# A list scheduler inside a kernel: a charge on vector work that overlaps GpSimd, and two GpSimd prices raised

## The chip, the cores and the metric

The kernel runs on one core of a Trainium2 chip. The metric is the device time of one execution in microseconds, from the first to the last instruction and what lies around them.

## The reference

Block-sparse attention, whose output is the input of a feed-forward layer with a rational function in place of an activation:

```
scores = scale * q @ k.T                    # batch 4, heads 8, sequence 768, head dim 64
mask   = own and neighbour blocks of 32, first and last block, 3 sampled blocks per row block
attn   = softmax(where(mask, scores, -1e9)) @ v
x      = attn as (3072, 512)
h      = x @ w_in                           # w_in 512 x 2048
P      = a0 + a1*h + a2*h^2 + a3*h^3
Q      = 1 + |b0|*|h| + |b1|*h^2
out    = (P / (Q + 1e-6)) @ w_out           # w_out 2048 x 512
```

`w_in` and `w_out` come as 64-bit floats.

## The kernel before

The 3072 tokens are cut into 12 chunks of 256 (three to a batch), the 2048 hidden values into 8 slices of 256. A **unit** is one chunk and one slice: 96 in all. The order of units is written out: slices 0 to 3 of chunk 0, slices 0 to 7 of chunk 1, slices 4 to 7 of chunk 0, and from there chunk by chunk. A unit's matmuls with `w_in` are lines 1036 to 1038 (function `into`, result `ph`), three passes since both sides are split into a high and a low half. ScalarE and VectorE then make the rational function (lines 1043 to 1081). Its value `gh` is written by VectorE at line 1071, and its remainder `gl` at line 1081. TensorE multiplies them with `w_out` (lines 1093, 1095 and 1099, result `acc`). So line 1093 of unit n waits for line 1071 of unit n.

Attention is done in parts of two row blocks (56 parts): scores on TensorE (line 817), mask and maximum on VectorE (829), exponentials on ScalarE (848), transposes of them (894), product with `v` (940), normalisation (966), transposes of the result (978), and its split into `xh` and `xl` (984 to 989). Four row-block pairs make a chunk. The first unit of a chunk needs the chunk's last `xl`.

The weights are decoded on the way. Each 64-bit word is loaded as two integers. A first copy of the high word (`convert`, line 437, by the helper at lines 150 to 154) goes to VectorE, ScalarE or GpSimd. Then VectorE alone does three integer steps (`pack1` to `pack3`, lines 441, 444, 447). For `w_out` (16 pieces, loaded at line 427 on SyncE's queue into two buffers `wl`) a high half `wo_h` (`out_high`), its remainder `wo_l` (`out_low`, line 461) and a short form `wo_b` (`out_short`) follow. For `w_in` (16 pieces) there are the largest value (378), the scale (344 to 356), the scaled copy `dw` (`scaled`), the high half (`high`) and the remainder (`low`, line 519). All of this is needed by the 12th unit.

What stands where in each engine's queue is set by a scheduler that runs while the program is built (`issue`). Every piece of work is an `Op` with an engine, or several to choose from (`among`), and a price in nanoseconds for each. The scheduler keeps a planned time for each engine, takes the operation that can start first, adds its price, and writes the instruction. Each engine then runs its queue in that order, whatever the real times are. Among engines, the home engine is preferred unless another can start earlier by a margin (`other`). While TensorE has nothing to do in the plan and no unit has been accumulated yet, `fill` writes a matmul without use (line 162) to its queue.

Of the kernel before, what the change touches and what calls it, by code (L numbers as in the profile page):

```python
# [24 lines left out]
def kernel(  # L25
# [71 lines left out]
    VE, SC, PO, TE, SY = "DVE", "Activation", "Pool", "PE", "SP"  # L97
# [17 lines left out]
    class Op:  # L115


        def __init__(self, eng, price, run, after=(), prio=0.0, takes=(), uses=(), unit=None, behind=None):
            self.alt = eng if isinstance(eng, dict) else None
            self.engs = list(eng) if self.alt else [eng]  # L120
            self.eng, self.price, self.run, self.prio, self.unit = self.engs[0], price, run, prio, unit
            self.after, self.behind = [a for a in after if a is not None], behind
            self.takes, self.uses, self.rings = list(takes), list(takes) + list(uses), {}
            for s in self.takes:
                self.rings[s.ring] = self.rings.get(s.ring, 0) + 1
            for s in self.uses:
                s.left += 1
            self.next, self.at, self.work = [], dict.fromkeys(self.engs, 0.0), 1.0
            plan.append(self)

    plan = []
# [10 lines left out]
    def among(key, home, **prices):  # L142

        d = {{"ve": VE, "sc": SC, "po": PO}[n]: p for n, p in prices.items()}
        return {home: d[home], **(d if key in ALT else {})}
# [18 lines left out]
    def issue(ahead):  # L164
# [11 lines left out]
        now = dict.fromkeys(todo, 500.0)  # L176
        clock, dma, lanes = -1.0, 0.0, [0.0] * 8
        busy, window, warm = {}, 0, False
        for n, o in enumerate(plan):
            o.n, o.wait = n, len(o.after) + (o.behind is not None)  # L180
            for a in o.after:
                a.next.append(o)
            if o.behind:
                o.behind.next.append(o)
            if not o.wait:
                for e in o.engs:
                    todo[e].append(o)
        left = len(plan)
        fsh = 0.8
        other = {VE: 500, SC: 534.0, PO: 243.0}  # L190
        unit_of = {VE: nc.vector, SC: nc.scalar, PO: nc.gpsimd}
        slack, fend, f00, fgap = 21.0, 80000, 3000, 0
        while left:
# [22 lines left out]
            if isinstance(price, list):  # L216
                for ns, size in price:
                    t = max(t, lanes.pop(0) if e == SY else t) + ns
                    dma = max(dma, t + 650) + size / 360.0
                    if e == SY:  # L220
                        lanes.append(dma + 900)
                end = dma + 900
            elif e == TE:
                f0 = max(now[e], f00)
                while f0 < fend and not accs:
                    tick(f0)
                    f = 213 if warm else 427
                    if f0 + f + fgap > t:
                        break
                    fill()  # L230
                    work_of(f0, f, 1.0)
                    f0 += f
                tick(t)
                if now[e] < fend and not accs:
                    w = window
                    x0 = w * 3413
                    for _ in range(2):
                        if not warm or t - x0 < 700 or busy.get(w, 0.0) >= fsh * (t - x0):
                            break
                        fill()  # L240
                        work_of(t, 213, 1.0)
                        t += 213
                if not warm:
                    price *= 2 if price > 1100 or price < 500 else 1.8
                work_of(t, price, o.work)
                end = t = t + price
            else:
                end = t = t + price
            now[e] = t
            o.end = end  # L250
# [146 lines left out]
    def weights():  # L397
# [21 lines left out]
        def one(prio, kind, u, x, before):  # L419
# [48 lines left out]
            before[kind] = o0  # L468
            w = [s_w] if kind else []
            o = Op(among("c", SC, sc=520, po=588, ve=335), 0, convert, [o0], prio, takes=w, uses=wl)  # L470
            if not kind:
                begun[u, x] = o
            o = Op(VE, 335, pack1, [o], prio, uses=w)
# [2 lines left out]
            if not kind:  # L476
                freed[u, x] = o
            if kind:
                o1 = Op(among("o", SC, sc=520, po=588, ve=335), 0, out_high, [o], prio, uses=w)
                o2 = Op(among("p", PO, po=1225, ve=602), 0, out_low, [o1] + homes(x), prio, uses=w)  # L480
                o3 = Op(among("q", SC, sc=520, po=588, ve=335), 0, out_short, [o] + homes(x), prio, uses=w)
                out_ready[x] = [o2, o3]
                decoded.append(o3)
                decoded.append(o2)
                return o2
# [10 lines left out]
    def w_scaled(u, prio, group, sums):  # L496
# [10 lines left out]
        for x in range(NCC):  # L507
            def three(x):
# [10 lines left out]
                    eng.tensor_tensor(out=wi[:, x, u, 1], in0=d["w"], in1=wi[:, x, u, 0], op=ALU.subtract)  # L519

                a = Op(among("s", PO, po=671, ve=396, sc=613), 0, scaled, [o], prio, takes=[s_ws])
                a = Op(among("h", SC, sc=520, po=588, ve=335), 0, high, [a], prio, uses=[s_ws])
                a = Op(among("l", PO, po=1113, ve=602), 0, low, [a], prio, uses=[s_ws])
                in_ready.setdefault(u, []).append(a)
                decoded.append(a)
            three(x)
# [719 lines left out]
```

## Time and profile before

| | |
|---|---|
| median of three runs | 829.0 us (827.88 to 829.31) |
| profiled execution: time, span from first to last instruction | 828.6 us, 826.8 us |
| TensorE busy | 770.6 us (93%) |
| VectorE busy | 674.9 us (82%) |
| ScalarE busy | 569.7 us (69%) |
| GpSimd busy | 107.5 us (13%), all in the first 220 us |

The profile page cuts the span into 40 slices of 20.7 us. TensorE's busy share is lowest in the sixth, VectorE's is highest from there to the eleventh, and from the twelfth on TensorE is at 9 tenths or more in every slice. The page's row for TensorE's granted clock shows less than full speed only in the fifth to seventh slice.

### The profile page before, as it was taken

To read this page: it belongs to the slowest core of one execution; us is meant where nothing else is said; L and a number is where in the kernel's file an instruction comes from. 1 tells how busy PE (TensorE), PEld (TensorE's weight loads), DVE (VectorE), ACT (ScalarE), POOL (GpSimd) and SP (SyncE) were. 2 spreads that over 40 slices of the span, in tenths; PEclk is the share of its full clock that TensorE was granted. 3 is DMA by queue.
4 is the path that set the end of the run, shared out by engine and by line. 5 is a ranking of instruction groups with operands and counts; after the bars stand their busy time and mean duration, and the time that the engine had idled before them with its cause. 6 is when DMAs were issued, how large, how long until landed. Compare 5 with 4: busy or idle time off the path is not lost.

```text
span 826.8 us, 27468 instructions
## 1 busy us (share of the span) xinstructions
PE 770.6 (93%) x10859; PEld 557.3 (67%) x10943; DVE 674.9 (82%) x1580; ACT 569.7 (69%) x1264; POOL 107.5 (13%) x149
## 2 busy tenths in 40 slices
PE   8798918898999999999999999999999999999997
PEld 4556605676677768677777767677777767767774
DVE  2788999899988885788878884887888886887886
ACT  2676777677866769677576759676676758766563
POOL 3547485613100000000000000000000000000000
PEclk9999969899999999999999999999999999999999
DMA  7988874537566957545636757635555436220000
GB/s 210 242 220 238 233 231 138 163 87 189 142 154 165 214 162 194 162 123 162 160 108 164 191 145 196 173 96 157 144 151 149 117 111 182 76 65 2 1 26 26
DMA packets 224416, 121.29 MB, mean 147 GB/s; under 512 B 62624, under 2 KB 214048, under 8 KB 224288
## 3 DMA queue, kind: packets, MB, share of 16 engines
q1 hardware_dynamic: 223136, 115.34, 51.6%
q0 software_dynamic: 1152, 4.19, 1.6%
q8 instruction: 86, 1.41, 0.8%
q14 instruction: 42, 0.34, 0.1%
HBM read 108.47 MB, written 11.01 MB: 145 GB/s over the span
## 4 chain that ended last, share of the span: by engine, by line
PE 81%; DVE 7%; DMA 4%; issue 3%; ACT 2%; POOL 2%; SPq 1%; ACTq 0%; POOLq 0%; DVEq 0%
PE acc L1093 11%; PE ph L1036 9%; PE acc L1095 9%; PE acc L1099 9%; PE ph L1037 9%; PE ph L1038 9%; PE m L817 7%; PE av L940 6%; PE m L894 6%; PE acc L162 3%; DMA vg<-in_v_dram 2%; PE m L556 2%; DMA wl<-in_moe_w_out_dram 1%; PE m L978 1%; POOL wo_h L154 1%
## 5 line engine op out<-in xcount | busy, mean ns | idle before, releaser
L1037 PE MATMUL ph<-xl,wi 128*128 128x256 f16 x768 | 210.5, 274 | 3.1 <-DVE xl L989 3.1
L1036 PE MATMUL ph<-xh,wi 128*128 128x256 f16 x768 | 210.9, 275 | 1.4 <-DVE tt L1053 1.4
L1038 PE MATMUL ph<-xh,wi 128*128 128x256 f16 x768 | 210.7, 274 | 0.0
L1043 ACT ACTIVATE sq<-ph,fc 128x512 f32<-128x512 f32 x96 | 65.9, 687 | 112.6 <-PE ph L1038 112.4
L1093 PE MATMUL acc<-wo_h,gh 128*128 128x512 f32 x384 | 114.5, 420 | 18.7 <-DVE gh L1071 18.0
L848 ACT ACTIVATE pr<-pr,st 128x256 f32<-128x256 f32 x224 | 110.7, 501 | 14.3 <-DVE st L860 14.3
L1060 DVE SCALAR_TENSOR_TENSOR ab<-sq,absb,ab 128x512 f32<-128x512 f32 x96 | 73.2, 763 | 37.1 <-ACT ab L1057 36.9
L829 DVE CUSTOM_DVE_ANT_1 pr<-m,bias 128x256 f32<-128x256 f32 x224 | 83.2, 418 | 22.3 <-PE m L817 22.1
L1099 PE MATMUL acc<-wo_b,gl 128*128 128x512 bf16 x368 | 95.4, 379 | 3.4 <-issue 2.1
L1095 PE MATMUL acc<-wo_l,gh 128*128 128x512 bf16 x316 | 86.5, 384 | 4.6
L1036 PEld LDWEIGHTS <-wi 128*128 128x128 f16 x768 | 75.9, 99 | 21.4 <-issue 5.1
L1071 DVE SCALAR_TENSOR_TENSOR gh<-tt,par,rr 128x512 fp32r<-128x512 f32 x96 | 72.3, 753 | 19.8 <-ACT rr L1067 11.2
L1093 PEld LDWEIGHTS acc<-wo_h,gh 128*128 128x128 f32 x384 | 66.0, 191 | 32.7 <-issue 19.6
L150 ACT ACTIVATE pT<-m 128x512 f32<-128x512 f32 x112 | 64.1, 596 | 34.0 <-PE m L894 32.7
L1037 PEld LDWEIGHTS <-wi 128*128 128x128 f16 x768 | 75.6, 98 | 12.7 <-issue 0.2
L1038 PEld LDWEIGHTS <-wi 128*128 128x128 f16 x768 | 75.5, 98 | 12.6 <-issue 3.4
L1047 ACT ACTIVATE tt<-ph,par,fc 128x512 f32<-128x512 f32 x96 | 74.8, 779 | 0.3 <-DVE gl L1081 0.2
L1050 DVE TENSOR_TENSOR tt<-tt,sq 128x512 f32<-128x512 f32 x96 | 66.9, 697 | 9.4 <-ACT tt L1047 9.4
L1057 ACT ACTIVATE ab<-ph,fc 128x512 f32<-128x512 f32 x96 | 65.6, 683 | 11.2 <-DVE tt L1077 10.5
L1077 DVE SCALAR_TENSOR_TENSOR tt<-tt,par,ab 128x512 f32<-128x512 f32 x96 | 72.2, 752 | 0.5
L894 PE MATMUL m<-ident,pr 128*128 128x128 f32 x448 | 69.6, 288 | 2.9 <-ACT kt L150 2.3
L1053 DVE SCALAR_TENSOR_TENSOR tt<-ph,fc,tt 128x512 f32<-128x512 f32 x96 | 71.4, 744 | 0.8
(130 smaller groups left out, 1221.7 us busy)
## 6 DMA issues: line engine op xcount, KB each, us to landing
vg<-in_v_dram SPq DMA_DIRECT2D x312, 64.0 KB, 2.9
vg<-in_v_dram SPq DMA_DIRECT2D x88, 192.0 KB, 3.6
kall<-ks SPq DMA_DIRECT2D x138, 64.0 KB, 1.9
wl<-in_moe_w_out_dram SPq DMA_DIRECT2D x16, 512.0 KB, 4.8
vg<-in_v_dram SPq DMA_DIRECT2D x12, 512.0 KB, 5.1
kall<-ks SPq DMA_DIRECT2D x23, 256.0 KB, 3.7
ldq<-in_q_dram SPq DMA_DIRECT2D x20, 256.0 KB, 3.4
out_dram<-ld SPq DMA_DIRECT2D x20, 256.0 KB, 2.4
```

The costliest lines, as they stand in the source:

```text
L829: nc.vector.tensor_tensor_reduce(out=prs[x][:, e, g].rearrange("p (s r) -> p s r", r=BLK), in0=h["sp"][g][:, e], in1=add.rearrange("p (s o ...
L848: nc.scalar.activation(out=prs[x][:, e, g], in_=prs[x][:, e, g], func=AF.Exp, scale=SCALE, bias=st[:, 12 + y:13 + y], accum_out=st[:, 16 + ...
L894: nc.tensor.transpose(pp[:, jj * P:(jj + 1) * P], pr[:, e, g, kt:NS * BLK:2], ident)
L1036: nc.tensor.matmul(o, wh, xh[:, :, cc], start=(cc == 0), stop=False)
L1037: nc.tensor.matmul(o, wh, xl[:, :, cc], start=False, stop=False)
L1038: nc.tensor.matmul(o, wl, xh[:, :, cc], start=False, stop=(cc == NCC - 1))
L1047: nc.scalar.activation(out=d["tt"], in_=d["ph"], func=AF.Identity, scale=d["cst"][:, 3:4], bias=par[:, 2:3])
L1060: nc.vector.scalar_tensor_tensor(out=d["ab"], in0=d["sq"], scalar=absb[:, 1:2], in1=d["ab"], op0=ALU.mult, op1=ALU.add)
L1071: nc.vector.scalar_tensor_tensor(out=d["gh"], in0=d["tt"], scalar=par[:, 0:1], in1=d["rr"], op0=ALU.add, op1=ALU.mult)
L1093: nc.tensor.matmul(acc, g, wo_h[:, f], start=(new and e == 0), stop=False)
L1095: nc.tensor.matmul(acc, g, wo_l[:, f], start=False, stop=False)
L1099: nc.tensor.matmul(acc, g, wo_b[:, f], start=False, stop=(last and e == 1))
```

## The change

The scheduler gets a list of GpSimd's planned operations on weights (`pooled`), each with a factor `drag`: 0.36 for copies, 0.62 for subtractions. An operation planned for VectorE gets longer by the factor times its overlap with such an operation (`dragged`). When GpSimd's operation is planned after VectorE's, VectorE's planned time is moved by the same product. Two prices on GpSimd rise: that of `out_high` from 588 to 1050, and that of `out_low` from 1225 to 1400. No instruction of the program changes by itself. What changes is which engine takes a weight operation, and the order in every queue.

```diff
+        pooled = []
+        def dragged(t, price):
+            more = 0.0
+            for a, b, drag in pooled:
+                more += drag * max(0.0, min(b, t + price) - max(a, t))
+            return more
...
             else:
+                if e == PO and o.drag:
+                    while pooled and pooled[0][1] < t - 20000:
+                        pooled.pop(0)
+                    pooled.append((t, t + price, o.drag))
+                    late = o.drag * max(0.0, min(now[VE], t + price) - max(t, last_dve))
+                    now[VE] += late
+                if e == VE:
+                    last_dve = t
+                    price += dragged(t, price)
                 end = t = t + price
...
             o = Op(among("c", SC, sc=520, po=588, ve=335), 0, convert, [o0], prio, takes=w, uses=wl)
+            o.drag = 0.36
...
-                o1 = Op(among("o", SC, sc=520, po=588, ve=335), 0, out_high, [o], prio, uses=w)
-                o2 = Op(among("p", PO, po=1225, ve=602), 0, out_low, [o1] + homes(x), prio, uses=w)
+                o1 = Op(among("o", SC, sc=520, po=1050, ve=335), 0, out_high, [o], prio, uses=w)
+                o2 = Op(among("p", PO, po=1400, ve=602), 0, out_low, [o1] + homes(x), prio, uses=w)
+                o2.drag = 0.62
...
                 a = Op(among("s", PO, po=671, ve=396, sc=613), 0, scaled, [o], prio, takes=[s_ws])
+                a.drag = 0.36
                 a = Op(among("h", SC, sc=520, po=588, ve=335), 0, high, [a], prio, uses=[s_ws])
                 a = Op(among("l", PO, po=1113, ve=602), 0, low, [a], prio, uses=[s_ws])
+                a.drag = 0.62
```

The changed file has more lines, so a line of the kernel before stands some 20 lines later in it: 1071 becomes 1093, 1093 becomes 1115.

How many weight operations each engine gets, counted in the built programs:

| operation | VectorE | ScalarE | GpSimd |
|---|---|---|---|
| first copy, `w_out` (`dw<-wl`) | 2, now 0 | 5, now 7 | 9, now 9 |
| first copy, `w_in` (`wi<-wo_l`, `wi<-wo_b`) | 3, now 2 | 6, now 5 | 7, now 9 |
| scaled copy (`dw<-wi,scw`) | 4, now 3 | 0, now 2 | 12, now 11 |
| high half of `w_out` (`wo_h<-dw`) | 2, now 1 | 6, now 9 | 8, now 6 |
| remainder of `w_out` (`wo_l<-dw,wo_h`) | 1, now 0 | 0 | 15, now 16 |

TensorE's queue gets 143 fills for 135. From the 25th unit on, the order of VectorE's and ScalarE's queue is that of before.

**TensorE, before the third unit's line 1093.** In the kernel before, the third unit's product with `w_out` stands right behind the second's:

```order
L556 MATMUL m_101<-ident,ldq 128x128 x4
L1099 LDWEIGHTS gl
L1099 MATMUL acc<-wo_b,gl 128x512
...
L1093 MATMUL acc<-wo_h,gh 128x512 x4
...
L894 MATMUL m_103<-ident,pr 128x128 x4
L894 MATMUL m_102<-ident,pr 128x128 x4
L894 MATMUL m_101<-ident,pr 128x128 x4
...
L940 MATMUL av<-vg_112,pT 32x64 x32
L339 MATMUL m_103<-ident,sums 128x128
```

In the changed kernel (line 916 is what 894 was, 962 what 940 was, 839 what 817 was):

```order
L1121 LDWEIGHTS gl
L1121 MATMUL acc<-wo_b,gl 128x512
L916 MATMUL m_103<-ident,pr 128x128 x4
L962 MATMUL av<-vg_112,pT 32x64 x32
L916 MATMUL m_103<-ident,pr 128x128 x8
L962 MATMUL av<-vg_110,pT 32x64 x32
...
L962 MATMUL av<-vg_112,pT 32x64 x32
L357 MATMUL m_102<-ident,sums 128x128
L839 MATMUL m_103<-kx,qt 32x96
...
L1000 MATMUL m_102<-ident,xn 128x128 x4
L1115 MATMUL acc<-wo_h,gh 128x512 x4
```

Three parts' transposes and products with `v`, one part's scores and the transposes of four blocks' output have moved ahead of the third unit's line 1093.

**VectorE, before the fifth unit's `gh`.** The names: `dw` and `wi` are weights being decoded, `fc` the coefficients of a slice, `xl` the low half of a chunk's input. Before:

```order
L1010 TENSOR_SCALAR fc<-wscale,sc_1035,par 128x2 x2
L989 SCALAR_TENSOR_TENSOR xl_119<-m_103,xscale,xh_118 128x512
L152 CAST wo_h<-dw 128x512
L461 TENSOR_TENSOR wo_l<-dw,wo_h 128x512
L154 TENSOR_SCALAR dw<-wi,scw 128x512 x2
L1060 SCALAR_TENSOR_TENSOR ab<-sq,absb,ab 128x512
L1050 TENSOR_TENSOR tt<-tt,sq 128x512
L1053 SCALAR_TENSOR_TENSOR tt<-ph,fc,tt 128x512
L154 TENSOR_SCALAR dw<-wl 128x512
L441 TENSOR_SCALAR dw<-dw 128x512
L1060 SCALAR_TENSOR_TENSOR ab<-sq,absb,ab 128x512
L1071 SCALAR_TENSOR_TENSOR gh<-tt,par,rr 128x512
```

In the changed kernel:

```order
L465 SCALAR_TENSOR_TENSOR wi<-wo_b,wi 128x512
L465 SCALAR_TENSOR_TENSOR wi<-wo_l,wi 128x512
L459 TENSOR_SCALAR wi<-wi 128x512
L1082 SCALAR_TENSOR_TENSOR ab<-sq,absb,ab 128x512
L462 SCALAR_TENSOR_TENSOR wi<-wo_b,wi 128x512
L1075 SCALAR_TENSOR_TENSOR tt<-ph,fc,tt 128x512
L465 SCALAR_TENSOR_TENSOR wi<-wo_b,wi 128x512
L851 ISA pr,st<-m_103,bias 128x256
L851 ISA st 128x1
L851 ISA pr,st<-m_101,bias 128x256
L851 ISA st 128x1
L1093 SCALAR_TENSOR_TENSOR gh<-tt,par,rr 128x512
```

The fifth unit's `gh` has moved ahead of the coefficients, of two `w_out` pieces' steps and of a third's first. From the fourth unit's `gh` to the fifth's there are 64 VectorE instructions before and 19 now. The `xl` of the second chunk stands 52 instructions earlier, ahead of the fourth unit's `gh`.

**SyncE's queue, the last two loads of `w_out` pieces.** Before (`kall<-ks` are loads of key blocks for a later part, `vg` of value blocks):

```order
L427 DMA wl<-in_moe_w_out_dram 128x1024
L912 DMA vg_110<-in_v_dram 48x8x128
L914 DMA vg_110<-in_v_dram 16x8x128
L915 DMA vg_110<-in_v_dram 16x8x128
...
L427 DMA wl<-in_moe_w_out_dram 128x1024
```

In the changed kernel:

```order
L445 DMA wl<-in_moe_w_out_dram 128x1024
L934 DMA vg_113<-in_v_dram 48x8x128
L936 DMA vg_113<-in_v_dram 16x8x128
L937 DMA vg_113<-in_v_dram 16x8x128
...
L797 DMA kall<-ks 128x4x128
L733 TENSOR_LOAD ix
...
L803 DMA kall<-ks 128x128
L445 DMA wl<-in_moe_w_out_dram 128x1024
```

The second of these is the sixteenth piece's load. It now stands behind these key loads of a part (one at line 797, six at line 803), which came after it before. The fourteenth piece's load stands behind two such groups, of which it was ahead before. In all, three groups stand ahead of the sixteenth load for one before.

## Rows read from the trace of the kernel before

**Rows 1.** Busy time of each engine in two stretches of the span.

```profile
core 0: us, PE busy (x) PEld busy (x) DVE busy (x) ACT busy (x) POOL busy (x), PEclk, DMA share, GB/s
85.00:225.00 140.00, 109.41 (x1756) 80.17 (x1765) 134.44 (x295) 103.22 (x230) 63.63 (x57) 0.91 0.60 168
225.00:826.80 601.80, 588.53 (x7781) 430.12 (x7852) 481.51 (x1094) 417.21 (x907) 0.00 (x0) 1.00 0.48 130
```

**Rows 2.** Timeline of TensorE: start, duration, instruction, idle time before it and releaser.

```profile
103.51 1.03 PE L1099 MATMUL acc<-wo_b,gl 128*128 128x512 bf16 x4
122.09 2.05 PE L1093 MATMUL acc<-wo_h,gh 128*128 128x512 f32 x4 [17.55 <-DVE gh L1071]
```

**Rows 3.** Busy time in two stretches of 5 us, columns as in the first group.

```profile
110.00:115.00 5.00, 0.00 (x0) 0.00 (x0) 3.23 (x4) 2.98 (x9) 4.92 (x5) 0.50 0.91 310
145.00:150.00 5.00, 2.37 (x12) 1.64 (x12) 3.61 (x8) 2.67 (x5) 3.50 (x5) 0.50 0.57 160
```

**Rows 4.** Timeline of GpSimd: instructions on weights.

```profile
82.21 0.62 POOL L154 TENSOR_SCALAR wo_h<-dw 128x512 fp32r<-128x512 f32 x1 [3.05 <-DVE dw L447]
...
101.42 7.89 POOL L154 TENSOR_SCALAR wo_h<-dw 128x512 fp32r<-128x512 f32 x1 [5.90 <-DVE st L860]
...
113.87 1.27 POOL L154 TENSOR_SCALAR dw<-wl 128x512 f32<-128x512 f32 x2
...
205.69 0.89 POOL L154 TENSOR_SCALAR dw<-wl 128x512 f32<-128x512 f32 x1 [4.05 <-DMA wl<-in_moe_w_out_dram]
```

**Rows 5.** Timeline of VectorE, five instructions.

```profile
114.55 0.87 DVE L441 TENSOR_SCALAR dw<-dw 128x512 int32<-128x512 int32 x1 [1.77 <-POOL dw L154]
...
125.03 0.74 DVE L1071 SCALAR_TENSOR_TENSOR gh<-tt,par,rr 128x512 fp32r<-128x512 f32 x1
...
146.84 0.74 DVE L989 SCALAR_TENSOR_TENSOR xl<-m,xscale,xh 128x512 f16<-128x512 f32 x1
...
157.86 0.77 DVE L1071 SCALAR_TENSOR_TENSOR gh<-tt,par,rr 128x512 fp32r<-128x512 f32 x1
...
208.91 0.83 DVE L441 TENSOR_SCALAR dw<-dw 128x512 int32<-128x512 int32 x1
```

**Rows 6.** Groups of instructions by line and tile: count, busy us, mean ns, idle before.

```profile
L154 POOL TENSOR_SCALAR wo_h<-dw 128x512 fp32r<-128x512 f32 x8 | 14.3, 1794 | 37.2 <-DVE dw L447 22.6 <-DVE st L872 8.7 <-DVE st L860 5.9
...
L154 DVE TENSOR_SCALAR dw<-wi,scw 128x512 f32<-128x512 f32 x4 | 4.9, 1239 | 3.4 <-POOL wi L519 2.0 <-POOL wo_l L461 1.4
L150 ACT ACTIVATE wo_h<-dw 128x512 fp32r<-128x512 f32 x6 | 3.8, 634 | 7.6 <-DVE dw L447 7.6
...
L154 DVE TENSOR_SCALAR dw<-wl 128x512 f32<-128x512 f32 x2 | 1.9, 956 | 0.0
...
L154 DVE TENSOR_SCALAR wi<-wo_l 128x512 f32<-128x512 f32 x2 | 1.2, 584 | 0.0
...
L152 DVE CAST wo_h<-dw 128x512 fp32r<-128x512 f32 x2 | 0.8, 404 | 0.0
L461 DVE TENSOR_TENSOR wo_l<-dw,wo_h 128x512 bf16<-128x512 f32 x1 | 0.7, 693 | 0.0
```

**Rows 7.** Waits of VectorE from 60 to 225 us: us, times, longest.

```profile
DVE dw L441 <- POOL dw L154: 2.0, 2, 1.8
```

**Rows 8.** Timeline of SyncE's queue: issue of the last piece's load and a key group.

```profile
199.20 0.36 SPq L427 DMA_DIRECT2D wl<-in_moe_w_out_dram  x1
...
204.13 0.43 SPq L775 DMA_DIRECT2D kall<-ks  x1
205.56 0.40 SPq L777 DMA_DIRECT2D kall<-ks  x1
207.48 3.38 SPq L781 DMA_DIRECT2D kall<-ks  x6
```

**Rows 9.** DMA issues of the page: KB each, median us from issue to landing.

```profile
wl<-in_moe_w_out_dram SPq DMA_DIRECT2D x16, 512.0 KB, 4.8
```

More of the change, by code (lines that the diff above doesn't have):

```diff
@@ L127, in __init__ @@
                 s.left += 1
-            self.next, self.at, self.work = [], dict.fromkeys(self.engs, 0.0), 1.0
+            self.next, self.at, self.work, self.drag = [], dict.fromkeys(self.engs, 0.0), 1.0, 0.0
             plan.append(self)
@@ L189, in issue @@
         fsh = 0.8
+        last_dve = 0.0
         other = {VE: 500, SC: 534.0, PO: 243.0}
```

## Prediction, on record before the run

> **What bounds the kernel now.** I read the busy time by stretch first. From 225 us to the end TensorE is busy 588.5 of 601.8 us at the full clock, and VectorE 481.5 [rows 1]. From there TensorE alone sets the time. From 85 to 225 us it is the other way round: VectorE is busy 134.4 of 140 us, TensorE only 109.4 [rows 1]. This is the stretch in which the weights are decoded beside the first units, and GpSimd works in no later one. So the end of the kernel moves by what VectorE's work in this stretch moves, as long as TensorE has idle time there to give up. It has 140 - 109.4 = 30.6 us.
>
> Second, TensorE's timeline shows where that idle time is. Its largest piece is 17.55 us ahead of the third unit's product with `w_out`, which waits for VectorE's `gh` [rows 2]. Behind that instruction in TensorE's queue stood transposes and products of attention that could have run. Within that idle time the granted clock is at 0.50, the lower of the two levels (1.2 GHz). It is there again around 147 us, where TensorE works less than half of the time [rows 3]. Four matmuls of line 1093 then take 2.05 us together [rows 2]. These holes cost nothing by themselves while VectorE is the bound. They are the room into which the other work can move.
>
> Third, GpSimd's timeline shows what its overlap with VectorE does. One copy to `wo_h` takes 7.89 us, another of the same kind 0.62 us [rows 4]. Behind the long one stands a first copy of weights (`dw<-wl`), for which VectorE then waits 1.77 us [rows 4, 5].
>
> **The change, part by part.** *Work taken from VectorE.* Six instructions leave it. By the groups' mean durations they are one `wo_h` cast at 0.40 us, one scaled copy at 1.24, two first copies of `w_out` at 0.96, one first copy of `w_in` at 0.58 and one remainder at 0.69 [rows 6]. That is 0.40 + 1.24 + 1.91 + 0.58 + 0.69 = 4.8 us. In a stretch where VectorE is busy 96% of the time I count all of it.
>
> *Who takes it.* ScalarE gets six operations more, at 0.63 us each as its `wo_h` copies show [rows 6], 3.8 us in all. It is busy 103.2 of 140 us there [rows 1], and this idle time hides them. Without that cover they would cost up to 3.8 us. GpSimd loses two `wo_h` copies and one scaled copy, and gets one remainder and two first copies more. That is within 2 us either way, under 63.6 busy us of 140 [rows 1]: nothing.
>
> *Waits that belong to removed instructions.* VectorE waited 2.0 and 1.4 us for GpSimd ahead of its two scaled copies near 150 us [rows 6]. These two instructions are no longer VectorE's. The bounds are 0, if what stands there next waits for the same thing, and 3.4 us. I take half, 1.7. VectorE's wait for `dw<-wl` was 2.0 us in two pieces, 1.8 of it at 114.55 us [rows 5, 7]. Between the long copy and that first copy GpSimd's queue holds as much work as before. It could vanish, or grow by as much, since VectorE now has less other work to do at that place. I count 0, bounds -1.8 to +1.8.
>
> *Order of VectorE's work.* From the fourth unit's `gh` to the fifth's there are 125.03 to 157.86, or 32.8 us, and 64 instructions; now there are 19 [rows 5]. The decoding behind them is not gone, it comes after. This gives TensorE the fifth to eighth units' work earlier, and the second chunk's `xl`, which came at 146.84 us [rows 5], before the fourth `gh`. It removes no VectorE work, so I cost it at 0. What it does is to fill TensorE's holes, and those have to shrink for VectorE's gain to reach the end. In TensorE's queue three parts' transposes and value products have moved ahead of the wait of 17.55 us [rows 2]. If the holes stayed, TensorE would still have to make up the gain after 160 us, where it is nearly always busy. Then up to all of the gain would be lost.
>
> *The eight more fills.* They are written while the plan has TensorE idle, early. Bounds: nothing if TensorE is idle there in fact, and a few us if not. The nearest row for a matmul of 512 columns at the full clock is the `gl` product, four in 1.03 us [rows 2], so eight take about 2 us. VectorE's queue and not TensorE's sets the stretch behind them: 0.
>
> *The queue of loads.* Here something is added. The sixteenth `w_out` piece was issued at 199.20 us [rows 8] and lands 4.8 us after it [rows 9]. GpSimd's first copy of it runs from 205.69 for 0.89 us [rows 4], and VectorE's first step starts at 208.91 [rows 5]. The slack is 208.91 - 206.58 = 2.3 us. Two key groups more now stand ahead of it. A group takes SyncE 0.43 + 0.40 + 3.38 = 4.2 us to issue [rows 8], so 8.4 us in all. If nothing else moved, VectorE would wait 8.4 - 2.3 = 6.1 us, and behind its waiting step stand the next units' `gh`, for which TensorE waits. The lower bound is 0: the groups wait for scores of the last part of the first batch, which now stand a unit earlier, and the whole queue shifts with the gain. I take a third, 2.0.
>
> *Sum.* 4.8 + 1.7 + 0 - 2.0 = 4.5 us. The span of 826.8 us becomes 822.3, and the profiled execution's 828.6 becomes 824.1. The median of the runs is 829.0, 0.4 above the profiled one. A time within 0.2% of the kernel before (1.7 us) can't be told from no change.
>
> **A rule against the trace.** The row shows 7.89 us for a copy that can take 0.62, while VectorE worked without a pause from 101.42 on [rows 4]. GpSimd lost its turn to a train of VectorE instructions, and the loss has nothing to do with a share of the overlap. The change charges a share, 0.36 or 0.62. By the row's mechanism the same copy meets the same train, since the decoding steps of the first `w_in` pieces behind it are still one block in VectorE's queue. The long copy then comes again, VectorE's wait behind it grows by 1.8 us, and the sum is 4.5 - 1.8 = 2.7 us, or 825.9 us. The Trainium skill, page "SBUF — State Buffer", section "Who interferes with whom", says that VectorE and GpSimd share a pair of ports by an exclusive lock: a VectorE instruction with two SBUF inputs and a GpSimd instruction that reads SBUF exclude each other, and whichever starts first keeps the other out until it ends. By that rule the cost depends on who starts first and not on the price, so the change would leave it where it is; the 7.89 us agree that one side was kept out for long, though not that it is for one instruction only.
>
> **The rivals.**
> *The starved copy again*, as just worked out: 825.9 us. The unchanged block speaks for it. Against it speaks that seven other copies of that kind took (14.3 - 7.89) / 7 = 0.9 us [rows 4, 6], so it needs a bad moment.
> *More than VectorE's removed work.* If the loads come in time, all of VectorE's idle time from 85 to 225 us (140 - 134.4 = 5.6 us) goes too, and both holes of TensorE are filled, then the gain is 4.8 + 5.6 = 10.4 us and the time 818.2. VectorE has 120 us of slack after 225 us [rows 1], so it could follow a TensorE that is still further ahead. Against it: a new order brings waits of its own.
> *No change to be measured.* What VectorE saves, it waits elsewhere: 827.0 to 830.3 us. This needs new waits of 3 us more than I took, or holes that stay.
> *The loads decide: slower.* The fourteenth and the sixteenth piece each wait 6.1 us or share a part of it, 6.1 to 12.2 us in all, 9.2 in the middle. Then 828.6 - 4.8 - 1.7 + 9.2 = 831.3 us. It makes the kernel slower by over 0.2% from a wait of 4.8 + 1.7 + 1.7 = 8.2 us on. The rows for it are the small slack of 2.3 us and the groups' length; against it, that the scores which release the groups come earlier.
>
> **How the numbers follow.** My forecast, a gain of 2 to 7 us without the long copy's growth: 0.37. The starved copy again: 0.15. More than VectorE's removed work: 0.19. No change: 0.13. Slower: 0.16. Faster by over 0.2% are the first three, 0.71. The likeliest case's own range is 821.5 to 826.6 us. For 8 in 10 I go from 816.5, which leaves out the smaller part of the larger gain, to 831, which leaves out half of the slower case.
>
> **What would show it.** Right: from 85 to about 220 us VectorE is still busy over 94%, its work there is some 5 us less, the wait of TensorE ahead of the third unit's `w_out` product is below 12 us, the fifth `gh` comes well before 157 us, and the stretch after the handover to TensorE is as long as before. Wrong: VectorE waits of several us for first copies of the last `w_out` pieces with the load as releaser, a GpSimd copy of 8 us or more with VectorE waiting behind it, or a new hole on TensorE after 160 us.

## The result, and the profile after

The changed kernel takes 834.6 us (median of 6 runs, 831.94 to 836.29), the kernel before 829.7 in the same comparison (6 runs, 827.88 to 831.36). The ratio is 1.006, with a 95% interval of 1.0045 to 1.0076: slower by 4.9 us where a gain of 4.5 was forecast, and outside the range. The profiled execution took 831.94 us, 3.3 more than the profiled one of before; their spans differ by 3.4.

Busy time by stretch of the changed kernel:

```profile
core 0: us, PE busy (x) PEld busy (x) DVE busy (x) ACT busy (x) POOL busy (x), PEclk, DMA share, GB/s
85.00:225.00 140.00, 110.32 (x1638) 79.28 (x1636) 132.85 (x276) 103.70 (x229) 57.77 (x57) 0.93 0.65 174
225.00:830.20 605.20, 598.33 (x7926) 433.23 (x7924) 484.40 (x1103) 419.20 (x911) 0.00 (x0) 1.00 0.47 128
...
175.00:225.00 50.00, 41.35 (x550) 28.45 (x549) 45.30 (x104) 36.01 (x76) 12.32 (x11) 0.93 0.70 172
```

Behind 225 us the stretch is 605.2 us long, 3.4 more than in [rows 1]: the whole loss is there at 225 us, and TensorE only carries it to the end. VectorE's work from 85 us on is 132.85 + 484.40 = 617.3 us, before 134.4 + 481.5 = 615.9 [rows 1]. The six instructions have left it, and none of their 4.8 us shows.

TensorE's waits from 85 to 225 us:

```profile
engine line waited for: us in total, times, longest us
PE ph L1058 <- DVE tt L1075: 8.8, 3, 6.3
PE m L916 <- ACT pT L150: 5.3, 3, 3.6
PE acc L1115 <- DVE gh L1093: 4.7, 4, 3.1
PE acc L1115 <- ACT wo_h L150: 2.4, 1, 2.4
```

The hole of 17.55 us [rows 2] is gone, as forecast, and the longest wait is 6.3 us. The clock in 110 to 115 us is 0.97 and in 145 to 150 us 0.62, where both were at 0.50 [rows 3]; but it is at 0.50 from 114.7 to 121.5 us instead. (The page of before shows the clock below 9 tenths in the sixth and eighth slice, not in the fifth to seventh.) The fifth unit's `gh` starts at 145.76 us instead of 157.86 [rows 5]. The table shows how that lead is lost; starts in us, of `gh` on VectorE and of the unit's product with `w_out` (line 1093, now 1115) on TensorE:

| | gh 5 | product 5 | gh 9 | gh 12 | product 12 | gh 13 | product 13 | product 26 |
|---|---|---|---|---|---|---|---|---|
| before | 157.86 | 160.13 | 180.89 | 211.95 | 216.12 | 222.96 | 226.13 | 334.03 |
| changed | 145.76 | 149.30 | 180.71 | 212.74 | 213.84 | 222.75 | 229.94 | 337.61 |
| changed, second profile | 146.53 | 150.52 | 183.19 | 216.28 | 218.06 | 226.28 | 235.61 | 343.46 |

A lead of 12 us at the fifth unit is used up by the ninth: work that was put off is done there. From `gh` 5 to `gh` 9 VectorE has 83 instructions, before 43. The 40 more are masks and sums of attention, coefficients, scales and steps of `w_out` parts. The loss appears between `gh` 9 and product 13, and from then on it stays nearly constant (3.8 us at product 13, 3.4 at the end). VectorE, at 200 to 214 us:

```profile
200.19 0.43 DVE L459 TENSOR_SCALAR dw<-dw 128x512 int32<-128x512 int32 x1 [1.09 <-POOL dw L154]
...
204.31 1.48 DVE L459 TENSOR_SCALAR dw<-dw 128x512 int32<-128x512 int32 x1 [1.07 <-POOL dw L154]
205.71 0.74 DVE L1093 SCALAR_TENSOR_TENSOR gh<-tt,par,rr 128x512 fp32r<-128x512 f32 x1
...
212.74 0.75 DVE L1093 SCALAR_TENSOR_TENSOR gh<-tt,par,rr 128x512 fp32r<-128x512 f32 x1
213.40 0.42 DVE L459 TENSOR_SCALAR dw<-dw 128x512 int32<-128x512 int32 x1
```

These waits are for GpSimd's first copies of the fourteenth and fifteenth `w_out` part, and GpSimd waits for their loads:

```profile
199.49 0.67 POOL L154 TENSOR_SCALAR dw<-wl 128x512 f32<-128x512 f32 x1 [3.59 <-DMA wl<-in_moe_w_out_dram]
203.63 0.65 POOL L154 TENSOR_SCALAR dw<-wl 128x512 f32<-128x512 f32 x1 [3.47 <-DMA wl<-in_moe_w_out_dram]
```

SyncE's queue issues them behind two key groups, and the sixteenth behind a third, at 207.88 us instead of 199.20 [rows 8]:

```profile
191.89 2.53 SPq L803 DMA_DIRECT2D kall<-ks  x5
194.54 0.36 SPq L445 DMA_DIRECT2D wl<-in_moe_w_out_dram  x1
...
198.81 0.36 SPq L445 DMA_DIRECT2D wl<-in_moe_w_out_dram  x1
...
204.78 2.99 SPq L803 DMA_DIRECT2D kall<-ks  x6
207.88 0.36 SPq L445 DMA_DIRECT2D wl<-in_moe_w_out_dram  x1
```

Behind VectorE's waiting steps stands the eleventh `gh`, for which TensorE waits at 206.60; then it waits for the sixteenth part's `wo_h`, which ScalarE could write only after the three steps that VectorE begins at 213.40:

```profile
206.60 1.82 PE L1115 MATMUL acc<-wo_h,gh 128*128 128x512 f32 x4 [3.14 <-DVE gh L1093]
...
217.00 1.15 PE L1115 MATMUL acc<-wo_h,gh 128*128 128x512 f32 x2 [2.35 <-ACT wo_h L150]
```

VectorE begins these three steps without waiting, right behind the twelfth `gh`: what makes them late is their place in its queue.

By the traces the two waits cost more than their length, since TensorE's clock falls behind them. Busy time from 200 to 225 us, of before, of the changed kernel, and of the changed kernel's second profile (run `after_again` below):

```profile
core 0: us, PE busy (x) PEld busy (x) DVE busy (x) ACT busy (x) POOL busy (x), PEclk, DMA share, GB/s
200.00:225.00 25.00, 22.63 (x351) 16.92 (x352) 25.00 (x57) 20.01 (x46) 6.57 (x6) 1.00 0.66 162
...
200.00:225.00 25.00, 19.51 (x224) 13.03 (x223) 22.48 (x48) 17.12 (x35) 4.59 (x5) 0.86 0.74 175
...
200.00:225.00 25.00, 18.19 (x155) 12.32 (x154) 20.65 (x42) 15.83 (x35) 5.09 (x5) 0.81 0.83 186
```

Before, the granted clock is 1.00 from 151 us to 826 us. In the changed kernel it is at 0.50, the lower level (1.2 GHz), from 206.9 to 210.3 us, after the wait that ended at 206.60, and from 217.1 to 220.5 us, after the one that ended at 217.00. TensorE is busy in all of these 6.8 us, and in 12.1 us at 0.50 behind the same two waits of the second profile. The four matmuls at 206.60 take 1.82 us; the same four take 1.19 us at the full clock, in a run shown below. If half of the busy time at 0.50 is lost, an estimate, that is 3.4 us in the first profile and 6.0 in the second. Product 13 is 3.8 us later than in the first profile of before, and in the second 9.1 later than in the second of before. No run took the clock's fall away by itself, so its price is read from the traces and not shown by an experiment.

The other thing to see is VectorE's instructions from 100 to 175 us. Five of the seven lines of a unit's work, by form (count | busy us, mean ns | idle before), first of before, then of after:

```profile
L1060 DVE SCALAR_TENSOR_TENSOR ab<-sq,absb,ab 128x512 f32<-128x512 f32 x7 | 5.8, 836 | 0.6 <-ACT ab L1057 0.6
L1077 DVE SCALAR_TENSOR_TENSOR tt<-tt,par,ab 128x512 f32<-128x512 f32 x6 | 4.5, 744 | 0.0
L1053 DVE SCALAR_TENSOR_TENSOR tt<-ph,fc,tt 128x512 f32<-128x512 f32 x6 | 4.4, 741 | 0.1
L1050 DVE TENSOR_TENSOR tt<-tt,sq 128x512 f32<-128x512 f32 x6 | 4.2, 697 | 0.0
L1081 DVE TENSOR_TENSOR gl<-tt,rr 128x512 bf16<-128x512 f32 x6 | 4.1, 679 | 0.0
```

```profile
L1099 DVE SCALAR_TENSOR_TENSOR tt<-tt,par,ab 128x512 f32<-128x512 f32 x7 | 6.8, 977 | 0.1
L1072 DVE TENSOR_TENSOR tt<-tt,sq 128x512 f32<-128x512 f32 x7 | 6.7, 956 | 0.0
L1082 DVE SCALAR_TENSOR_TENSOR ab<-sq,absb,ab 128x512 f32<-128x512 f32 x6 | 6.0, 1004 | 0.0
L1103 DVE TENSOR_TENSOR gl<-tt,rr 128x512 bf16<-128x512 f32 x6 | 5.6, 940 | 0.0
L1075 DVE SCALAR_TENSOR_TENSOR tt<-ph,fc,tt 128x512 f32<-128x512 f32 x6 | 4.4, 736 | 0.0
```

The same instructions are up to 261 ns longer, apart from the one that reads `ph`. The two lines that are not shown, `gh` and line 1074 (now 1096), grow by some 100 ns. I summed over all of VectorE's instructions how much longer each is than the median of its group where no GpSimd instruction of over 0.3 us overlaps it. From 100 to 175 us that is 10.7 us before and 16.1 after. Three more traces of the order before give 9.4 to 11.0, and five more of the order after 15.1 to 16.2. The sums depend on how instructions are grouped: other groupings give 9.6 to 11.7 and 15.7 to 16.2 for the first two traces. Some 5 us of VectorE's time are lost to GpSimd that were not lost before, as much as the removed instructions saved. In the whole run the sums are 26.7 and 29.5. That the overlap with GpSimd makes the difference is read from these rows.

### The profile page after: what moved, and what is told of

It reads as the page before. It is cut to its first block, busy times and chain, and to the rows that moved or that the text cites. A ratio compares the mean times of both kernels' runs of the same rounds, so it can differ in the third digit from the quotient of the medians.

```text
span 830.2 us, 27576 instructions
## 1 busy us (share of the span) xinstructions
PE 782.5 (94%) x10951; PEld 559.4 (67%) x10951; DVE 675.0 (81%) x1574; ACT 573.6 (69%) x1270; POOL 101.9 (12%) x149
## 4 chain that ended last, share of the span: by engine, by line
PE 78%; DVE 12%; DMA 3%; issue 2%; ACT 2%; SPq 1%; POOL 0%; ACTq 0%; POOLq 0%
PE acc L1115 10%; PE acc L1117 9%; PE acc L1121 9%; PE ph L1058 9%; PE ph L1060 9%; PE ph L1059 9%; PE m L839 7%; PE av L962 5%; PE m L916 5%; PE acc L162 3%; PE m L578 1%; DVE tt L1099 1%; PE m L1000 1%; DMA vg<-in_v_dram 1%; DMA wl<-in_moe_w_out_dram 1%
## 5 line engine op out<-in xcount | busy, mean ns | idle before, releaser
L1121 PE MATMUL acc<-wo_b,gl 128*128 128x512 bf16 x384 | 98.7, 379 | 3.0 <-DVE gl L1103 2.3
L1117 PE MATMUL acc<-wo_l,gh 128*128 128x512 bf16 x384 | 101.5, 387 | 0.0
L1099 DVE SCALAR_TENSOR_TENSOR tt<-tt,par,ab 128x512 f32<-128x512 f32 x96 | 75.9, 791 | 0.7
L1072 DVE TENSOR_TENSOR tt<-tt,sq 128x512 f32<-128x512 f32 x96 | 68.7, 716 | 9.4 <-ACT tt L1069 9.4
L916 PEld LDWEIGHTS m<-ident,pr 128*128 128x128 f32 x448 | 63.2, 205 | 15.0 <-ACT pT L150 7.0
```

The costliest lines, as they stand in the source:

```text
L916: nc.tensor.transpose(pp[:, jj * P:(jj + 1) * P], pr[:, e, g, kt:NS * BLK:2], ident)
L1099: nc.vector.scalar_tensor_tensor(out=d["tt"], in0=d["tt"], scalar=par[:, 0:1], in1=d["ab"], op0=ALU.add, op1=ALU.subtract)
L1117: nc.tensor.matmul(acc, g, wo_l[:, f], start=False, stop=False)
L1121: nc.tensor.matmul(acc, g, wo_b[:, f], start=False, stop=(last and e == 1))
```

## The experiments

The theories. **A**, and later **E**: the late loads of the last `w_out` parts cost the time. **B**: it is GpSimd's lengthening of VectorE's instructions. **C**: a lag of 2.5 us that VectorE has at 45 us, where every engine's queue is still as before. **D**: the places of the last parts' steps in the engines' queues. Each ratio is to the kernel before, with its 95% interval.

**Each half of the change alone.** `prices_only` has the new prices and `o.drag = 0.0` in all four places, `drag_only` the old prices (`po=588`, `po=1225`) and the shares.

> The two raised prices alone, all factors of the charge zero. The order is one of its own. If the charge on VectorE is what pushes decoding work behind the units, this one should look like the kernel before around the third unit (a TensorE wait of over 12 us there), and be within 1 us of its 829.7 us. Theory A has it slower only if its sixteenth load is issued later than 203 us; theory B only if VectorE's instructions between 100 and 175 us are lengthened by over 13 us in all.

> The charge alone, with the two old prices. If the charge makes the loss, this is as slow as the changed kernel, 833 to 836 us, whatever the prices. Theory A has it slow only with the sixteenth load issued later than 203 us; theory B only with VectorE lengthened by over 13 us between 100 and 175 us.

Measured: 832.7 us, 1.0033 [1.0015, 1.0052], and 831.6 us, 1.0029 [1.0017, 1.0042]. Both forecasts of the time missed: `prices_only` was to stay within 1 us of 829.7, and `drag_only`, if the charge makes the loss, was to take 833 to 836 us. Either half makes it slower by about half of the loss. Neither alone is the cause. The sixteenth load is issued at 204.26 and 205.02 us in them, later than 203 us, as theory A asks.

**The loads put ahead in the changed order, and put back in the order before.** All other queues stay as they are.

```
loads_first (of after):
+  HOLD = {14: 14, 15: 16, 16: 16}   # key load of a part waits for that many wl loads
...
+  if wl_n[0] < HOLD.get(x, 0): held[x] = load
+  else: load()
loads_last (of before):
+  WAITS = {14: 1, 16: 2}            # wl load waits for that many key groups
...
+  held.append((WAITS.get(x + 1, 0), load_now))
```

> The changed kernel, with one difference: the key loads that stand ahead of the fourteenth and the sixteenth w_out load on SyncE's queue are held back until those loads are issued, in the order that the kernel before had. All other queues are those of the changed kernel. Theory A (the late loads cost the time): the sixteenth load is issued some 7 us earlier than at 207.9 us, the wait of 2.35 us of TensorE for the last wo_h goes, and the time falls by 3 to 5 us, to 830 to 831.5 us. Theory B (VectorE loses more to GpSimd in the new order, 16 us between 100 and 175 us for 11): the loads are early but VectorE is not, and the time stays within 1 us of the changed kernel's 834.6. Theory C (the changed kernel already lags by 2.7 us at 45 us, where no queue differs, for a reason that is not the order): stays as well, and the lag at 45 us is there or not in each run whatever the kernel.

> The mirror of the run with the loads first: the kernel before, with its fourteenth w_out load held back behind one group of key loads, and the sixteenth behind two, and nothing else changed. Theory A: the last load is late by 7 us or more, VectorE waits 3 to 5 us for it, and the time rises by 3 to 5 us, to 832.5 to 834.5. Theory B and theory C: less than 1.5 us, since the other engines' queues are those of before.

Measured: `loads_first` 835.3 us, 1.0072 [1.0057, 1.0088], no better than the change. `loads_last` 834.8 us, 1.0073 [1.0051, 1.0094]. So late loads do cost the order before 5 us, with no byte more or less to move. In the changed order this edit wins nothing back, but it put only two loads ahead, and by little: the fourteenth is issued at 191.69 us for 194.54, the sixteenth at 205.68 for 207.88, and the fifteenth, behind a key group and value loads, at 201.85, later than the 198.81 above. GpSimd's timeline in `loads_first` (line 161 is the changed kernel's 154, 157 its 150):

```profile
206.58 0.67 POOL L161 TENSOR_SCALAR dw<-wl 128x512 f32<-128x512 f32 x1 [6.38 <-ACT wo_h L157]
```

This is the copy of the fifteenth part. The row names ScalarE's `wo_h`, which ended at 206.43 us; the fifteenth load landed at 206.44, so the row can't tell which of them it waited for last. Moving SyncE's queue alone moved the wait, and the run does not settle what early loads would be worth.

**Both kernels once more, and both with GpSimd's subtractions cut.**

```
small_sub (of before, of after), in out_low and likewise in low:
+  to = 32 if eng is nc.gpsimd else DM
+  eng.tensor_tensor(out=wo_l[:, x, 0:to], ...)
+  if to < DM: eng.memset(wo_l[:, x, to:DM].bitcast(F32), 0.0)
```

> The kernel before, unchanged, profiled once more. In the first profile TensorE waited 2.62 us at 23.4 us with nothing named as the cause ('issue'), and the granted clock stayed at 1.00 after it; in the changed kernel the same place took 3.17 us, the clock fell to 0.50, and VectorE was 2.5 us late by 45 us although every engine's queue is the same up to there. If the lag belongs to the kernel (theory C): 2.3 to 2.7 us again, clock 1.00. If it differs from run to run (rival): a wait anywhere from 2.3 to 3.7 us, and the lag with it. Span 826 to 829 us under both.

> The changed kernel, unchanged, profiled once more. Theory C (the lag belongs to the kernel): the wait at 24 us is over 3.0 us again, clock 0.50 behind it, VectorE 2 to 3 us behind the kernel before at 45 us. Rival (run to run): 2.3 to 3.7 us, perhaps no fall of the clock, and the lag gone. Theory B (GpSimd lengthens VectorE's instructions more in the new order): the excess of VectorE's instructions over their lengths without GpSimd, 16.1 us in 100 to 175 us in the first profile against 10.7 before, comes again within 1.5 us.

> The kernel before, in which each subtraction that the planner gave to GpSimd works on 32 of its 512 columns and a memset fills the others with zeros (so part of the low halves of the weights is left out); the plan and every queue's order stay. Theory B: VectorE is lengthened less, 3 to 8 us faster than before (822 to 827). If the lengthening does not reach the end: within 2 us of before.

> The changed kernel with the same cut: GpSimd's subtractions on 32 of 512 columns, zeros in the others. Theory B (the changed order loses 5.4 us more to GpSimd's subtractions on VectorE): the distance between the two orders, 4.9 us uncut, shrinks to under 1.5 us, or turns. Theory D (the changed order is itself worse: steps of the last pieces stand later on VectorE, and its waits at 175 to 225 us remain): the distance stays at 3.5 us or more. Theory C alone: 2 to 3 us stay.

Measured: 828.8 and 837.7 us, one run each. In the second profile of the changed kernel the early wait is 2.62 us, as short as in the first of before, and in the second of before it is 2.89; yet the changed kernel's span is 836.0 us. VectorE's lag at 45 us is then 0.2 us between the two second profiles. So C falls. The cut kernels take 821.7 us, 0.9908 [0.9892, 0.9923], and 830.7 us, 1.0027 [1.001, 1.0044]. The distance between the orders does not shrink, it grows from 4.9 to 9.0 us: B alone falls too. Something else holds the changed order, which taking lengthening away doesn't reach. (By the two ratios the distance is 9.9 us. The medians come from different sessions, in which the kernel before took 828.5 to 829.7 us.)

**The last four loads left out.**

```
loads_gone (of before, of after):
+  if kind and x > 11:
+      d["ld"] = last_wl[0]     # the twelfth part's buffer
+      return
```

> The kernel before without the w_out loads of the last four parts: their steps decode the rows of the twelfth part once more, out of its buffer (so the last four parts' weights are wrong); the plan and every engine's order stay. Theory E (the late loads of the last parts are what the changed order loses by): little to win here, 0 to 3 us faster than before. Theory D (the places of the last parts' steps in VectorE's and GpSimd's queues): the same, 0 to 3 us.

> The changed kernel without the same four loads. Theory E (late loads): the distance between the orders, 4.9 us with the loads, falls under 1.5 us, so this gains 3.5 us or more beyond what loads_gone_before gains; the waits of VectorE for GpSimd's copies at 200 and 204 us (2.2 us) and of TensorE for gh at 206 us (3.1 us) are gone. Theory D (places in the queues): the distance stays at 3.5 us or more, and TensorE still waits for the sixteenth part's wo_h at about 215 us.

Measured: 829.8 us, 1.0006 [0.9993, 1.0018], and 830.5 us, 1.0013 [1.0001, 1.0025]. The distance falls to 0.7 us. E holds: the loads cost the changed order 4.1 us and the order before nothing. All six runs of the changed kernel lie above all twelve of this one. These runs take the loads' traffic away together with their lateness; that lateness is enough to cost 5 us, `loads_last` shows. D's sign is there too: TensorE still waits for the sixteenth part's `wo_h`, 2.57 us at 216.30.

**One and two of these loads left out** (`x == 15`, and `x in (13, 14)`, in place of `x > 11`, counted from 0).

> The changed kernel without the w_out load of the sixteenth part alone (its steps decode the rows of the fifteenth part once more). With all four of the last loads away it took 830.5 us, with them 834.6. If the sixteenth load, issued at 207.88 instead of 199.20 us, is the one that costs: 830 to 832 us. If the fourteenth and fifteenth (194.54 and 198.81 us) hold VectorE up, through GpSimd's copies: 833.5 to 835.5 us. If both do: 832 to 833.5.

> The changed kernel without the w_out loads of the fourteenth and fifteenth parts alone (their steps decode the rows of the thirteenth). If these hold VectorE up: 830 to 832 us, and VectorE's waits for GpSimd's copies at 200 and 204 us (2.2 us) and TensorE's for gh at 206 us (3.1 us) are gone. If it is the sixteenth: 833.5 to 835.5 us, with TensorE's wait for wo_h at 217 us in place. If both do: 832 to 833.5.

Measured: 837.1 us, 1.0106 [1.0083, 1.0128], and 833.7 us, 1.0062 [1.0048, 1.0077]. Neither alone wins anything. (`gone_16` stands 2.5 us above the changed kernel's median, 0.6 below its second profile. In its trace TensorE is busy at 0.50 for 9.4 us behind the two waits, for 6.8 and 12.1 in the changed kernel's profiles.) TensorE's timeline in `gone_16`, then in `gone_14_15`, then with all four away (line 1120 is the changed kernel's 1115, and 1098 its 1093):

```profile
209.45 1.22 PE L1120 MATMUL acc<-wo_h,gh 128*128 128x512 f32 x4 [4.29 <-DVE gh L1098]
219.55 0.73 PE L1120 MATMUL acc<-wo_h,gh 128*128 128x512 f32 x2 [2.00 <-ACT wo_h L150]
```

```profile
217.43 1.22 PE L1120 MATMUL acc<-wo_h,gh 128*128 128x512 f32 x2 [5.15 <-ACT wo_h L150]
```

```profile
206.33 1.19 PE L1120 MATMUL acc<-wo_h,gh 128*128 128x512 f32 x4
...
216.30 1.22 PE L1120 MATMUL acc<-wo_h,gh 128*128 128x512 f32 x2 [2.57 <-ACT wo_h L150]
```

Without the sixteenth load both waits stay, 4.29 and 2.00 us. Without the fourteenth and fifteenth the first is gone, but the second, for the sixteenth part's `wo_h`, grows from 2.35 to 5.15 us: VectorE then waits 2.49 us for that part's first copy. The waits stand one behind the other, and the second hides what the first costs. With all four away the first is gone and the second stays at 2.57. An estimate of the first one's price is its 3.14 us and 1.7 us of work lost at the lower clock behind it, 4.8 in all, near the 4.1 measured.

**Both cuts together.**

> The kernel before with both cuts: the w_out loads of the last four parts left out (their steps decode the twelfth part's rows again) and GpSimd's subtractions on 32 of 512 columns, zeros in the others. The cuts alone gave 829.8 and 821.7 us; the loads bound nothing in this order, so 820 to 824 us under every theory.

> The changed kernel with both cuts; alone they gave 830.5 and 830.7 us. Theory F (two causes, which hide each other: the late loads cost some 4 to 5 us, and GpSimd's subtractions, which lengthen VectorE's instructions by 5 us more in 100 to 175 us than in the order before, took back what was saved on VectorE): with both away the forecast gain appears, 2 to 6 us less than both_before, so 815 to 821 us. Theory G (the saving on VectorE is worth nothing in this order, whatever the lengthening, since TensorE and ScalarE are waited for instead): within 1.5 us of both_before or above it.

Measured: 821.7 us, 0.9916 [0.9896, 0.9935], and 823.5 us, 0.9927 [0.9907, 0.9947]. The forecast gain does not appear: G, not F. (By the two ratios the distance is 0.9 us, and their intervals overlap.) Together:

| | order before | changed order | distance |
|---|---|---|---|
| whole | 829.7 | 834.6 | 4.9 |
| last four loads away | 829.8 | 830.5 | 0.7 |
| subtractions cut | 821.7 | 830.7 | 9.0 |
| both | 821.7 | 823.5 | 1.7 |

Down the columns: the loads cost the changed order 4.1 us, and 7.2 with the subtractions cut; they cost the order before nothing. Cutting the subtractions is worth 8.0 us before, and in the changed order 3.9 with the loads there and 7.1 without. In the changed order with both cuts VectorE is busy 124.43 of the 140 us from 85 on, and its longest waits, from 85 to 232 us, are:

```profile
DVE gh L1104 <- ACT rr L1100: 6.5, 4, 3.3
DVE xn L999 <- PE av L973: 5.0, 3, 3.6
DVE st L905 <- ACT pr L881: 2.8, 3, 2.1
```

**The last four parts due earlier in the changed order.** The planner then places their loads ahead of the key groups but one, and their VectorE steps earlier.

```
+  pieces = [(p - 1.0 if kind and x > 11 else p, kind, u, x) for p, kind, u, x in pieces]   # or 1.5
```

> The changed kernel, in which the planner gets a due time 1.0 unit earlier for the last four parts of w_out (their loads, copies and VectorE steps): their loads stand ahead of the key groups but one, and their steps two units earlier on VectorE; the order up to there stays. If the loss lies in the last parts (theories D and E): the loss of 4.9 us shrinks to between -3 and 2 us (827 to 832). If it lies ahead of them: 833 us or more.

> The same with 1.5 units: the VectorE steps of the last four parts stand where the kernel before has them or ahead. Theories D and E: 825 to 831 us, the lead of 10 us at unit 5 is kept in part. If the loss lies ahead of the last parts: 833 us or more. If a lead that VectorE gains is given back whatever comes first: as the kernel before within 2 us.

Measured: 832.0 us, 1.004 [1.0025, 1.0056], and 833.0 us, 1.0046 [1.0028, 1.0064]; the first is at the edge of its forecast (827 to 832 us), the second is a miss. TensorE no longer waits for the sixteenth part's `wo_h`, but `gh` 9 comes 3.3 and 4.5 us later than before. VectorE is busy 24.5 and 25.0 of the 25 us from 175 on, so I take it that steps put ahead for one unit delay another. No version that does all of the work beat the kernel before.

## Why the prediction was wrong, point by point

**What bounds the kernel: half right.** TensorE sets the time from 225 us on, VectorE is busy 96% of the time from 85 to 225 us [rows 1]. The step that failed is the conclusion that the end moves by what VectorE's work in the stretch moves. Cutting the subtractions took 26.7 - 10.5 = 16.2 us of lengthening off VectorE in the order before, and GpSimd's own work became shorter as well; the end moved by 8.0. In the changed order with the loads away it took 29.7 - 9.2 = 20.5 us, and the end moved by 7.1. By these two rates, a third to a half, 4.8 us of VectorE's time would be worth 1.6 to 2.4, an estimate. What the sum left out besides: it priced a wait at its length, and here TensorE's clock fell behind two of TensorE's waits. Of the signs named, VectorE's share (132.85 of 140 us, 94.9%), the closed hole and the early fifth `gh` came; 5 us less work on VectorE and an unchanged stretch after the handover did not.

**Work taken from VectorE, 4.8 us: the count right, the gain not there.** The six instructions are gone, and as much came back in longer instructions. I had priced GpSimd's part at nothing because its own time was to move by 2 us at most; what changed is which VectorE instructions stand beside it. That this lengthening took the gain is read from the traces. The cuts do not show it as the only cause, since without it the gain still doesn't appear, and other waits do.

**Waits at removed scaled copies, 1.7 us: right in their place.** I misread one of the two: the 2.0 us stood at 150.65 us, the 1.4 us at 68.49, outside the stretch. VectorE's waits list for 85 to 225 us no longer has the first. It has others: 2.2 us for first copies of `w_out`, 2.4 for `av`, 1.4 for `xh`, 6.8 us in all with the small ones, for 5.3 before.

**ScalarE's six operations and eight more fills, nothing: not contradicted.** ScalarE is busy 103.7 us of 140, as before. No run takes the fills away alone.

**Order of VectorE's work, 0: wrong in sign for the end of the stretch.** The holes closed as forecast, and the fifth `gh` comes 12 us early, though the fourth comes 5.7 us late (130.72 for 125.03). But the sixteenth part's steps, which began at 208.91 us ahead of the twelfth `gh` [rows 5], now begin at 213.40 behind it. With all four loads away `gh` 13 is 3.3 us ahead (222.03 against 225.32, the two `loads_gone` traces), close to the forecast gain. Product 13 is 0.7 us late (229.24 against 228.50), since TensorE has waited 2.57 us for that part's `wo_h` meanwhile, and its clock was at 0.50 from 216.1 to 219.5 us, 3.2 us of them busy, an estimated 1.6 us lost. The lead is lost there.

**The queue of loads, -2.0 us: the mechanism right, the size off.** It is -4.1 us. I had priced the sixteenth load alone, from its slack of 2.3 us. (It landed at 205.55 us, 6.4 after its issue; 4.8 is the median of all sixteen. The slack does not use it.) The fourteenth and fifteenth were late as well, by way of GpSimd's copies, and hold `gh` 11 up.

**The rivals.** *The starved copy* did not come: GpSimd's six `wo_h` copies take 0.94 us on average. It needs no bad moment, as I had argued: in all four traces in which the order before runs with its subtractions whole it takes 7.88 or 7.89 us. On the ports the unit's rows shown go with the rule: the lines that grew read two SBUF operands, and the one that didn't, 736 ns for 741, reads `ph`, which is in PSUM. That is what the Trainium skill, page "SBUF — State Buffer", section "Who interferes with whom", says of two SBUF inputs. A step with one input, on `wi` (line 441, now 459), grew too, from 482 to 577 ns, while the same step on `dw` shrank from 557 to 492. *The loads decide* is the rival that came nearest: 831.3 us forecast, 834.6 measured, with 4.1 us of late loads in place of 9.2, and the 6.5 us of savings absent. (The likeliest case's own range begins at 828.6 - 7 = 821.6 us, not at 821.5.)

**What stays open.** Why the 4.5 us don't appear with both cuts: the waits for ScalarE and TensorE that stand in VectorE's timeline there say what it waits for, but no run took them away. The clock is at 0.50 from 209.1 to 212.5 us there, after a wait of 2.24 us for the sixteenth part's `wo_h`, and at 1.00 in that place in the order before; this too is only read.

## What to carry to other kernels

An engine's busy share of 96% still gives no rate of exchange: time taken off VectorE here was worth a third to a half of its length, so test the rate by cutting something on the engine before adding up instructions. When an order moves, follow each load, copy and step of the last pieces through every queue to the instruction that is waited for, and price all pieces, not the last one: of two waits in a row one can hide the other, and taking the loads of either away shows nothing. Price a wait with the granted clock behind it, not by its length alone. A price that makes a planner avoid an overlap at one place moves the overlap to other instructions; look at their mean durations by form in both traces.

## What the runs showed of the hardware that was not expected

TensorE's waits at 206 and 217 us and the lower clock behind them stand above. By the same estimate the clock accounts for most of what sets the changed kernel's two profiles apart, 830.2 and 836.0 us. Up to product 13 TensorE is idle for 40.6 and 39.2 us in them, and busy at 0.50 for 22.3 and 33.4; half of that difference is 5.6 us.

TensorE stands still in the middle of one part's scores at about 23 us, waiting for nothing that the profile names. Of before, and of after:

```profile
25.98 0.60 PE L817 MATMUL m<-kall,qt 64*32 64x96 f32 x34 [2.62 <-issue]
```

```profile
27.13 0.85 PE L839 MATMUL m<-kall,qt 64*32 64x96 f32 x33 [3.17 <-issue]
```

A block of instructions lands by DMA 1.4 us before it goes on in both traces, so I take it for a wait for instructions. Over 18 traces with the same order up to there it lasts 1.52 to 3.72 us; in the kernel before it took 2.62 and 2.89, in the changed one 3.17 and 2.62. In 13 of the 18 the granted clock falls to 0.50 during it or right behind it, among them the changed kernel's second profile; the first of before, with the same 2.62 us, keeps 1.00. It belongs to neither order. Whether it is part of why runs of one kernel differ by 2 to 3 us, no run tested.
